# Three of a block's sixteen sums of silu(h) on GpSimd instead of VectorE, in a fused convolution and feed-forward kernel

## The chip, the cores and the metric

The kernel runs on one core of one Trainium2 chip. The metric is the device time of one execution in microseconds (us), inputs and outputs in the chip's main memory (HBM). A core has five engines that each work through their own list of instructions in order and meet only at semaphores: TensorE (PE in the profile; PEld is its loading of weights), VectorE (DVE), ScalarE (ACT), GpSimd (POOL) and SyncE (SP), which issues transfers. ScalarE and GpSimd can issue transfers too. Operands lie in SBUF, and TensorE's results in the eight banks of PSUM.

## What is computed

A light-weight convolution along the sequence with seven taps per head, softmax over the taps, and behind it a feed-forward layer with silu, all in float32:

```python
# x: 8 x 4096 x 192, weight: 8 heads x 7 taps
w = softmax(weight, axis=-1)
out[b, s, h, g] = sum over k of w[h, k] * x_pad[b, s + k, h, g]   # 6 zeros ahead of each sequence
# x = out as 32768 x 192; w_in: 192 x 2048, w_out: 2048 x 192
h = x @ w_in
g = h * (1.0 / (1.0 + np.exp(-h)))
return g @ w_out
```

## The kernel before

**Tiles.** The 32768 tokens are worked in NB = 32 blocks of 1024, each as two halves n of 512. The 192 features are three parts k of 64, and the 2048 hidden features are four groups j, each of two chunks a, with e the two 128-row pieces of a chunk. SBUF tiles of g (the silu of h) are [128, n, e, 512], one for each j and a.

**Fewer products.** From block 1 on the kernel doesn't multiply plainly. The up product (x @ w_in) is made of 15 products a group in place of 18 (`product`, L649, tokens P), whose right operands are sums of the block's features (`win`) and whose left operands are sums of the weights made at the start. ScalarE copies one accumulator out of PSUM (L698, tokens u), VectorE adds others to it (L692, tokens X, a, b), and ScalarE takes the silu (L710, tokens S). The down product (g @ w_out) is made in the same spirit, of seven forms in place of eight (`out_slot`, L765). Four of the forms need sums of g, made by `sum_g` (L733), four for each group j, so sixteen a block:

- t.j0 = g[0,1] - g[0,0], t.j1 = g[1,1] - t.j0, t.j2 = g[1,1] - g[0,1], t.j3 = g[1,0] - t.j1, where g[a,n] is chunk a, half n. Each is a subtraction of 128x1024 values.
- t.j0 and t.j1 share a tile `t`, t.j2 and t.j3 the next one. The pool of these tiles has three buffers.

The output products are tokens Di.je: slot i (0 to 5), group j, piece e. A slot is four products of 32 columns side by side. Slot 3 reads t.j2 (three of the four products) and t.j3, slots 4 and 5 read t.j0 and t.j3 and t.j3 alone, slot 2 reads t.j1, and slots 0 and 1 read g. So D3.00 and D3.01 are the readers of t.02, D3.10 and D3.11 of t.12, D3.21 and D3.20 of t.22.

**The convolution.** Taps of part k are tokens v.ki, i the tap (`conv`, L508 to L516), two blocks ahead of the output products that they stand among. Tap 0 is written by ScalarE (L508). For i from 1 to 6 and blocks from 4 on, ScalarE multiplies the shifted features by the tap into a buffer `u` (L511), and GpSimd issues a transfer that adds this buffer to the tile `nat` (L512, 256 KB read and written). Taps of one part add into the same tile, so each of these issues waits for the landing of the one before it in its part; and it waits in GpSimd's queue. A block has 18 of them. GpSimd also copies the six columns of the block before (`halo_in`, L498, or sets them to zero, L492). After the start it has no other work.

**The order.** `PLAN` is a list written out by hand: for every block, the tokens in the order in which they go to the engines' queues; a sign shifts a token to the block before (-) or after (+). `step` turns a token into instructions, and `pin` keeps their order in each queue. Only a few, the halo copy among them, are placed by the scheduler. `START` is the like list for the first block of this kind. The part of `PLAN` with the sums reads:

```
-P8.3 P5.0 v.02 -D1.00 =st.3 -t.00 -b5.3 -a0.2 -a0.3 -sp.2 -D1.30 u5.4 -a0.1 -D1.01
v.22 v.12 -D0.00 -S0.3 v.23 -D0.31 -D1.10 -t.01 -t.03 -D2.00 -sp.0 -b5.2 -t.02 -D4.01
-S1.2 -S5.2 -D5.00 -D2.01 v.03 -D5.01 -D3.00 -S0.1 -t.10 -D1.20 -D4.00 v.13 v.24
-D3.01 -t.11 -D2.11 -D2.10 -t.13 -D5.11 v.14 -D4.10 v.04 -D0.21 -S1.3 -w.0 -w.1 -S0.2
v.25 -t.20 -S5.4 -t.21 -D5.10 -D4.11 +ld.2 -D1.21 -D0.30 -D0.11 -t.23 -S5.3 -D4.20
-D5.20 -t.12 -D3.10 -D3.11 -D2.21 -D2.20 -D0.20 -D4.21 -t.22 -D3.21 v.05 -D1.31 -D5.21
-t.30 -D0.01 -w.2 -t.31 -t.33 -D5.31 -D1.11 v.15 v.26 +i.2 u5.0 -D0.10 -z1.0 -t.32
```

Ahead of it stand v.01, v.10 and v.11, and before these, at the end of the list, +v.21. The last block's output products are in `finish`.

Of the kernel before, what the change touches and what calls it, by code (L numbers as in the profile page):

```python
# [12 lines left out]
ALU = mybir.AluOpType  # L13
# [4 lines left out]
def kernel(  # L18
# [24 lines left out]
    nc = tc.nc  # L43
# [13 lines left out]
    NB = NT // TT  # L57
# [109 lines left out]
    def pin(ins):  # L167
        return tc.keep_in_program_order(ins)
# [549 lines left out]
    def sum_g(b, j, i):  # L718

        t = sums.setdefault((b, j), {})  # L720
        if i // 2 not in t:
            t[i // 2] = tpool.tile([P, 2, 2 * TB], F32, tag="t", name="t")

        def of(a, n):
            return gs[b, j, a][:, n, :, :].rearrange("p e t -> p (e t)")

        u, v = (
            (lambda: (of(0, 1), of(0, 0))),
            (lambda: (of(1, 1), t[0][:, 0, :])),
            (lambda: (of(1, 1), of(0, 1))),  # L730
            (lambda: (of(1, 0), t[0][:, 1, :])),
        )[i]()
        pin(nc.vector.tensor_tensor(t[i // 2][:, i % 2, :], u, v, op=ALU.subtract))  # L733

    def out_slot(b, j, i, e, half=None):

# [145 lines left out]
    def step(b, token):  # L882
# [19 lines left out]
        elif name[0] in "uXabS":  # L902
            sums_h(b, name, *digits)
        elif name == "t":
            sum_g(b, *digits)
        elif name[0] == "D":
            i, (j, e) = int(name[1]), digits
            for half in range(2) if i == 3 and b == NB - 1 else (None,):
                out_slot(b, j, i, e, half)
        elif name[0] in "Mzyx":  # L910
            merge(b, name, *digits)
        elif name == "o":
            turn_out(b, *digits)
        elif name == "st":
            store_out(b, *digits)
        elif name == "dp":
            next(downs)
        elif name == "cp":
            copy_plain(b, *digits)
        elif name == "go":  # L920
            pool.tensor_copy(warm, nats[1][:, digits[0], 0, 0:1])
            for g in (2, 3):
                for e in range(2):
                    combine(g, e)
        elif name == "ld":
            if b + 1 < NB:
                load(b + 1, digits)
        elif b + 1 < NB:
            {"i": turn_in, "ha": halo_in, "v": conv, "sp": spread, "w": win}[name](
                b + 1, *digits[: 1 + (name == "v")]  # L930
            )
# [204 lines left out]
```

## Time and profile before

| | |
|---|---|
| two timed runs | 2319.44 and 2320.99 us, median 2320.22 |
| span of the profiled execution | 2317.9 us |
| time of a block, from its first output product to the next block's | 71.19 us (blocks 5 to 29) |
| of it, output products | 36.2 us |
| busy: TensorE, VectorE, ScalarE, GpSimd | 2310.2, 1797.9, 1496.0, 534.9 us |
| sums (L733) | 496, 1.22 us each, all on VectorE |
| accumulating transfers (L512) | 504, 4.5 us from issue to landing in the median |

In the profile's rows a group of instructions is given by line, engine, operation and tiles (out<-in), and xN is their number. Timeline rows begin with the start and the duration in us from the start of the span; equal neighbours are merged, and in brackets stands how long the engine had been idle before and what ended that. A product in float32 has two records, so one Di.je is eight records. "PEclk" is the clock that TensorE was granted, as a share of full speed. In a row for a stretch of time the busy times of PE, PEld, DVE, ACT and POOL follow each other, then come PEclk, the transfers' share and GB/s.

### The profile page before, as it was taken

How to read it: one execution, taken by the hardware profiler on the slowest of the kernel's cores; microseconds unless marked ns; L12 is line 12 of the kernel's file. 1: busy time of each engine (PE TensorE's matmuls, PEld its weight loads, DVE VectorE, ACT ScalarE, POOL GpSimd, SP SyncE). 2: the span in 40 equal slices, each digit the busy share in tenths (PEclk: the TensorE clock that was granted, in tenths of full speed). 3: DMA queues.
4: the chain of work that ended last, by engine and by line, in shares of the span. 5: the costliest groups of instructions: out<-in, count | busy, mean ns of one | idle time of the engine just before them, and what ended most of it. 6: DMA issues, size and time to landing. Idle time of an engine off the chain costs nothing.

```text
span 2317.9 us, 45421 instructions
## 1 busy us (share of the span) xinstructions
PE 2310.2 (100%) x17630; PEld 949.6 (41%) x17630; DVE 1797.9 (78%) x2373; ACT 1496.0 (65%) x2779; POOL 534.9 (23%) x675
## 2 busy tenths in 40 slices
PE   9999999999999999999999999999999999999999
PEld 5454443444433344433444334443334443344433
DVE  8998777777777777777777777777777777777777
ACT  5347766677666686666776667866667666677543
POOL 4921112221122211222211222112221212221100
PEclk9999999999999999999999999999999999999999
DMA  7236557766567765677655676556776557765401
GB/s 159 58 62 101 98 100 118 123 115 102 95 113 120 121 105 93 109 120 121 110 98 99 115 124 117 102 93 113 119 123 108 94 104 120 120 114 93 81 17 25
DMA packets 522601, 238.81 MB, mean 103 GB/s; under 512 B 430368, under 2 KB 435488, under 8 KB 522384
## 3 DMA queue, kind: packets, MB, share of 16 engines
q0 software_dynamic: 73120, 133.89, 34.4%
q1 hardware_dynamic: 447392, 101.78, 25.0%
q8 instruction: 138, 2.26, 0.4%
q14 instruction: 79, 0.65, 0.1%
q10 hardware_dynamic: 1872, 0.23, 0.1%
HBM read 31.46 MB, written 25.17 MB: 24 GB/s over the span
## 4 chain that ended last, share of the span: by engine, by line
PE 89%; DVE 0%; issue 0%; ACT 0%; ACTq 0%
PE ps L765 45%; PE ps L649 39%; PE ps L666 5%; DVE cmb L175 0%; ACT u L175 0%; DVE osb L175 0%; ACTq L175 0%
## 5 line engine op out<-in xcount | busy, mean ns | idle before, releaser
L512 POOL DMA_DIRECT2D nat<-u x504 | 432.6, 947 | 1544.6 <-ACT u L511 1192.3
L765 PE MATMUL ps<-g,wo 128*32 128x512 f32 x2976 | 694.9, 592 | 0.0
L649 PE MATMUL ps<-win,wr 64*128 64x512 f32 x1550 | 688.7, 591 | 0.8 <-ACT yx L828 0.8
L649 PE MATMUL ps<-win,ws 64*128 64x512 f32 x1550 | 644.3, 589 | 0.0
L698 ACT COPY u<-ps 128x512 f32<-128x512 f32 x775 | 452.2, 587 | 166.8 <-PE ps L649 93.8
L765 PE MATMUL ps<-t,wo 128*32 128x512 f32 (+2 forms) x4528 | 538.5, 446 | 0.0
L765 PE MATMUL ps<-t,wx 128*32 128x512 f32 x2976 | 485.1, 592 | 0.0
L649 PE MATMUL ps<-dup,wr 64*128 64x512 f32 x868 | 425.6, 589 | 0.0
L511 ACT ACTIVATE u<-xt,taps 128x512 f32<-128x512 f32 x504 | 346.0, 715 | 44.0 <-DMA nat<-u 43.6
L733 DVE TENSOR_TENSOR t<-g,t 128x1024 f32<-128x1024 f32 x248 | 303.3, 1223 | 89.7 <-PE ps L765 84.2
L692 DVE TENSOR_TENSOR g<-u,ps 128x512 f32<-128x512 f32 x465 | 312.2, 682 | 72.2 <-PE ps L649 58.8
L649 PEld LDWEIGHTS ps<-win,wr 64*128 64x128 f32 x1550 | 275.7, 187 | 217.1 <-issue 177.1
L733 DVE TENSOR_TENSOR t<-g 128x1024 f32<-128x1024 f32 x248 | 298.8, 1216 | 76.4 <-PE ps L765 56.7
L692 DVE TENSOR_TENSOR ps<-u,ps 128x512 f32<-128x512 f32 x310 | 215.7, 696 | 132.3 <-PE ps L649 62.0
L710 ACT ACTIVATE g<-ps 128x512 f32<-128x512 f32 x465 | 281.0, 604 | 48.6 <-PE ps L649 47.0
L649 PEld LDWEIGHTS ps<-win,ws 64*128 64x128 f32 x1550 | 258.8, 187 | 126.1 <-issue 103.9
L710 ACT ACTIVATE g<-g 128x512 f32<-128x512 f32 x465 | 281.4, 629 | 30.3 <-DVE g L692 30.3
L765 PEld LDWEIGHTS ps<-t,wo 128*32 128x32 f32 x4528 | 181.4, 110 | 239.2 <-issue 227.6
L649 PE MATMUL ps<-dup,ws 64*128 64x512 f32 x682 | 271.9, 589 | 0.0
L831 ACT COPY cmb<-ps 96x512 f32<-96x512 f32 x30 | 17.4, 581 | 393.1 <-PE ps L765 393.1
L765 PE MATMUL ps<-g,wx 128*32 128x512 f32 x1488 | 245.9, 594 | 0.0
L765 PEld LDWEIGHTS ps<-g,wo 128*32 128x32 f32 x2976 | 170.4, 110 | 130.6 <-issue 129.8
(93 smaller groups left out, 2015.1 us busy)
## 6 DMA issues: line engine op xcount, KB each, us to landing
nat<-u POOLq DMA_DIRECT2D x504, 256.0 KB, 4.5
dup<-nat SPq DMA_DIRECT2D x345, 128.0 KB, 2.5
nat<-in_x_dram SPq DMA_DIRECT2D x382, 64.0 KB, 4.4
out_dram<-osb SPq DMA_DIRECT2D x376, 64.0 KB, 2.0
raw<-in_moe_w_out_dram SPq DMA_DIRECT2D x8, 384.0 KB, 3.7
raw<-in_moe_w_in_dram SPq DMA_DIRECT2D x12, 192.0 KB, 4.8
ws<-wr POOLq DMA_DIRECT2D x8, 192.0 KB, 4.8
raw<-in_moe_w_in_dram SPq DMA_DIRECT2D x6, 128.0 KB, 3.1
```

What stands on the lines that cost most here:

```text
L511: pin(nc.scalar.activation(z, src, AF.Copy, scale=tap))
L512: pin(nc.gpsimd.dma_start(out=dst, in_=z, accum_op=ALU.add))
L649: nc.tensor.matmul(to[:, cols], raw(g, *LEFT[e][r], e), rhs[:, cols], start=first, stop=True, skip_group_check=True,)
L666: nc.tensor.matmul(plain_bank(b, n and 1 + e)[:, cols], rows(wr[j] if own == e else ws[j], e)[:, a, k, :], rows(dups[b], e)[:, SLOT[e][2 * ...
L692: pin(nc.vector.tensor_tensor(out_, u, v, op=op))
L698: pin(nc.scalar.copy(us[b, g, o][:, cols], t1[:, cols]))
L710: pin(nc.scalar.activation(h, src, AF.Silu))
L733: pin(nc.vector.tensor_tensor(t[i // 2][:, i % 2, :], u, v, op=ALU.subtract))
L765: nc.tensor.matmul(accs[b][at][SQ * q : SQ * q + SQ, to], lhs[:, e, SQ * k : SQ * k + SQ], rhs[:, e, ts(q, TB // 4) if i == 5 else to], st ...
L831: pin(nc.scalar.copy(c[0], acc[0][0:n, :]))
```

## The change

In `sum_g` the sums t.02, t.12 and t.22 (i == 2, groups 0 to 2) of blocks 2 to 30 go to GpSimd. Their tokens keep their places in the list, and nothing else is changed.

```diff
@@ sum_g
             (lambda: (of(1, 1), of(0, 1))),
             (lambda: (of(1, 0), t[0][:, 1, :])),
         )[i]()
-        pin(nc.vector.tensor_tensor(t[i // 2][:, i % 2, :], u, v, op=ALU.subtract))
+        engine = nc.gpsimd if 1 < b < NB - 1 and i == 2 and j != 3 else nc.vector
+        pin(engine.tensor_tensor(t[i // 2][:, i % 2, :], u, v, op=ALU.subtract))
```

After the edit the lines behind L733 have numbers higher by one: the sums are L734, the output products L766. GpSimd's queue of one block reads, from the changed program: v.21, v.01, v.11, v.02, v.22, v.12, v.23, t.02, v.03, v.13, v.24, v.14, v.04, v.25, t.12, halo copy, t.22, v.05, v.15, v.26, v.06, v.16.

## The prediction

> **What bounds the kernel now.** I read the page first, then the waits of the changed line, then the timelines of TensorE, GpSimd and VectorE over one block.
>
> ```profile
> span 2317.9 us, 45421 instructions
> PE 2310.2 (100%) x17630; PEld 949.6 (41%) x17630; DVE 1797.9 (78%) x2373; ACT 1496.0 (65%) x2779; POOL 534.9 (23%) x675
> PE 89%; DVE 0%; issue 0%; ACT 0%; ACTq 0%
> ```
>
> TensorE bounds it: busy 2310.2 of 2317.9 us, and the chain that ended last is TensorE nearly throughout. No other engine sets the pace, so taking work from VectorE can bring at most the 7.7 us that TensorE is not busy. The changed line says the same from its side:
>
> ```profile
> L733 DVE TENSOR_TENSOR t<-g x248: 1181/1218/1227, 139.0 to 2295.1; 128x1024 f32<-128x1024 f32 x124
> who waited for it (us, times):
>   ACT nat L508: 6.1, 1
>   PEld ps L765: 1.2, 4
> ```
>
> A sum takes VectorE 1.22 us, and in the whole run TensorE waited 1.2 us for sums. What counts is whether GpSimd delivers the three sums before TensorE asks for them. This is block 15: TensorE's first output product (D1.00), then the first products that need t.02, t.12 and t.22 (D3.00, D3.10, D3.21); then VectorE's sums; then GpSimd's queue.
>
> ```profile
> 1136.90 0.63 PE L765 MATMUL ps<-g,wx 128*32 128x512 f32 x3
> 1145.09 1.04 PE L765 MATMUL ps<-t,wo 128*32 128x512 f32 x8
> 1156.90 1.04 PE L765 MATMUL ps<-t,wo 128*32 128x512 f32 x8
> 1162.05 1.04 PE L765 MATMUL ps<-t,wo 128*32 128x512 f32 x8
> ```
>
> ```profile
> 1141.60 1.22 DVE L733 TENSOR_TENSOR t<-g 128x1024 f32<-128x1024 f32 x1
> 1144.77 1.23 DVE L733 TENSOR_TENSOR t<-g,t 128x1024 f32<-128x1024 f32 x1
> 1147.90 1.23 DVE L733 TENSOR_TENSOR t<-g,t 128x1024 f32<-128x1024 f32 x1 [1.91 <-PE ps L765]
> ```
>
> ```profile
> 1132.46 0.88 POOL L512 DMA_DIRECT2D nat<-u  x1 [12.97 <-ACT u L511]
> 1137.35 2.60 POOL L512 DMA_DIRECT2D nat<-u  x3 [4.01 <-ACT u L511]
> 1143.53 0.86 POOL L512 DMA_DIRECT2D nat<-u  x1 [3.58 <-ACT g L710]
> 1146.61 1.72 POOL L512 DMA_DIRECT2D nat<-u  x2 [2.23 <-ACT u L511]
> 1148.95 0.84 POOL L512 DMA_DIRECT2D nat<-u  x1 [0.61 <-ACT g L710]
> 1155.46 2.59 POOL L512 DMA_DIRECT2D nat<-u  x3 [3.39 <-DMA nat<-u]
> 1157.08 1.19 POOL L498 COPY xt<-tail 64x18 f32<-64x18 f32 x1
> ```
>
> The sum t.02 is done on VectorE at 1142.82, 2.27 us before D3.00 at 1145.09. GpSimd is only 23% busy, but its queue is in order, and it is a queue of waits: each accumulating transfer of the convolution (L512) waits until the one before it in its feature part has landed. In the order of the list the issues are v.21, then v.01 (1132.46); v.11, v.02, v.22 (the three from 1137.35); v.12 (1143.53); v.23 and v.03 (the two from 1146.61); v.13 (1148.95); v.24; and v.14, v.04, v.25 (the three from 1155.46), then the halo copy. The token -t.02 stands between v.23 and v.03, -t.12 behind v.25, and -t.22, as the changed program's GpSimd queue has it, behind the halo copy and ahead of v.05.
>
> **The change part by part.** It moves 87 sums: three in each of blocks 2 to 30. Tiles, readers and the instruction orders of TensorE, ScalarE and SyncE stay.
>
> Removed from VectorE: 87 x 1.22 = 106 us of busy time. This is worth nothing: TensorE waited 1.2 us for sums in all, so I count a gain of 0.
>
> The price of one sum on GpSimd. The trace has no subtraction of 1024 elements there, but it has smaller ones, undisturbed, one behind the other:
>
> ```profile
> 111.75 0.45 POOL L175 TENSOR_TENSOR ws<-wr,ws 64x128 f32<-64x128 f32 x1
> 112.17 0.45 POOL L175 TENSOR_TENSOR ws<-wr 64x128 f32<-64x128 f32 x1
> 120.74 0.60 POOL L175 TENSOR_TENSOR wx<-wo,wx 128x192 f32<-128x192 f32 x1
> 121.29 0.60 POOL L175 TENSOR_TENSOR wo<-wo 128x192 f32<-128x192 f32 x1
> ```
>
> From start to start that is 0.42 us at 128 elements and 0.55 at 192: 0.13 per 64. Carried on to 1024 (832 more than 192, 13 times 64) it is 0.55 + 13 x 0.13 = 2.24; the spans (0.45, 0.60) give 0.60 + 13 x 0.15 = 2.55. Bounds: not under VectorE's own 1.22, not over 0.55 x 1024/192 = 2.93, where nothing would be fixed cost. I take 2.3, nearest to the start-to-start slope.
>
> Sum t.02. It starts when the issue of v.23 is over, 1146.61 + 0.86 (the row of v.12 has 0.86 for one issue) = 1147.47, and ends at 1149.77. D3.00 wanted it at 1145.09: TensorE stands 4.68 us in this block, and everything behind it in TensorE's order with it. Nothing earlier in the block moves, since v.23 hangs on v.22's landing, and v.22 on ScalarE's work of the block's up products, all before the stall. So the stall comes anew in each block that still has transfers in the queue, and that is blocks 2 to 29: the 504 issues below, 18 a block; in block 30 nothing stands ahead of t.02. The mean over those 28 pairs of rows, (start of v.23) + 0.84 + 2.3 - (start of D3.00), is 4.86; the first and the last pair are these, and give 5.59 and 3.87.
>
> ```profile
> nat<-u POOLq DMA_DIRECT2D x504, 256.0 KB, 4.5
> ```
>
> ```profile
> 218.30 1.04 PE L765 MATMUL ps<-t,wo 128*32 128x512 f32 x8
> 220.75 1.72 POOL L512 DMA_DIRECT2D nat<-u  x2 [3.50 <-ACT u L511]
> 2141.72 1.04 PE L765 MATMUL ps<-t,wo 128*32 128x512 f32 x8
> 2142.45 1.73 POOL L512 DMA_DIRECT2D nat<-u  x2 [2.74 <-ACT u L511]
> ```
>
> 28 x 4.86 = 136 us. With the bounds 1.22 and 2.93 of one sum it is 106 to 154.
>
> Sum t.12. Behind t.02 wait v.03 and v.13: issued at 1149.8 and 1150.3, so v.13 is 1.4 later than before; v.14, which waits for v.13's landing, goes from 1155.46 to 1156.8, v.25 behind it is over at 1158.05 + 1.4 = 1159.4, and t.12 ends at 1161.7. D3.10 now asks at 1156.90 + 4.68 = 1161.6. That is a tie; over the blocks I count 0.1 each, 3 us (bounds 0 and 1.3, if every landing slips as far as v.13's issue).
>
> Sum t.22. The halo copy ends 1158.27 - 1158.05 = 0.2 after the last issue, so t.22 ends near 1161.7 + 0.2 + 2.3 = 1164.2; D3.21 asks at 1162.05 + 4.8 = 1166.9. Hidden by 2.7 us. What is queued behind it, v.05 and its kind, moves by less than TensorE does, so the next block sees it no later.
>
> VectorE during t.02: its next sum, t.13 at 1147.90, waits for TensorE (D4.00, which stands behind D3.00) and slides with the stall, so after 1146.00 VectorE does nothing that could disturb GpSimd. Count 0.
>
> The clock. A stall of 4.9 us is new to this kernel, and TensorE's clock answers to idleness. At the end of the run TensorE's last work ends at 2307.32 + 4.92 = 2312.24, and the clock falls:
>
> ```profile
> 2307.32 4.92 PE L765 MATMUL ps<-t,wo 128*32 128x512 f32 x97
> 2313.00:2318.00 5.00, 0.00 (x0) 0.00 (x0) 1.28 (x4) 0.37 (x1) 0.00 (x0) 0.82 0.40 66
> 1.14 3.78 PE L435 MATMUL ps<-zeros 128*128 128x256 f32 x8 [1.14 <-DVE warm L175]
> 5.25 1.16 PE L435 MATMUL ps<-zeros 128*128 128x256 f32 x4
> ```
>
> The granted clock (the column of 0.82) means 1.8 of those 5 us at 0.5, so it fell at 2316.2, after 3.9 us of idleness. At the start of the run the same matmuls take 0.47 us each (3.78/8) and later 0.29 (1.16/4): TensorE is slow for about 4.1 us (1.14 to 5.25) after a rest. A fall would thus cost half of 4.1 us, 2.05. One fall after 3.9 us does not tell how often a stall of 3.9 to 5.6 brings one; the bounds are none and all 28 (0 and 57 us), and I take the middle, 29. The Trainium skill (TensorE: Matmul & The Clock Gate, Part 1) says that the gate looks at free-running windows of about 3.4 us and halves the clock after an idle one. By it a stall of 4.9 us holds a whole window in (4.9 - 3.4)/3.4 = 44% of its positions, 12 of 28 blocks, an estimate of 25 us in place of 29; the 3.9 us of the row agree with it.
>
> The sum: 2317.9 + 136 + 3 + 29 = 2486 us of span. The two timed runs have a median of 2320.2, 2.3 above this profiled execution's span, so 2488.
>
> **The rivals.**
> (a) The clock never falls: the stalls are too short or fall badly for it. For it speaks that the only fall seen came at 3.9 us, not below; against it that most stalls here are longer. 2320 + 139 = 2459.
> (b) The clock falls in every block: 2320 + 139 + 57 = 2516.
> (c) VectorE and GpSimd keep each other out of SBUF. At the start of the run this is visible: the same 64x128 operation that takes 0.45 us alone takes 1.17 beside a VectorE operation of 1.21.
>
> ```profile
> 46.91 1.17 POOL L175 TENSOR_TENSOR wr<-wr,ws 64x128 f32<-64x128 f32 x1
> 45.42 1.21 DVE L175 SCALAR_TENSOR_TENSOR two<-raw,two 128x768 int32<-128x768 int32 x1
> ```
>
> Were t.02 and t.12 each held for one VectorE sum (1.22), that is 28 x 2.44 = 68 us more, and the longer stalls would fetch the clock down nearly always: 2516 + 68 = 2584. Against it stands that VectorE itself waits for TensorE while t.02 runs. The Trainium skill (SBUF — State Buffer, Who interferes with whom) says that a VectorE instruction with two SBUF inputs and a GpSimd one that reads SBUF exclude each other for the whole instruction; the row agrees.
> (d) Not slower: v.22 lands early, so that v.23 leaves early. This one place decides: v.22, the third of the issues from 1137.35 to 1139.95, begins at about 1139.1, and a landing takes
>
> ```profile
> DMA to landing us min/median/max: 3.2/4.5/8.2
> ```
>
> 3.2 us at least. v.23 at 1142.3 would still end t.02 at 1145.4, 0.35 after D3.00: 28 x 0.35 = 10 us, 2330. To cost nothing, v.23 must leave before 1141.9. Against it: v.23 leaves after D3.00 began in the blocks shown, first and last included.
>
> **How the numbers follow.** The stall with some falls of the clock 0.58 (own range 2465 to 2512), (a) 0.18, (b) 0.12, (c) 0.07, (d) 0.05. The forecast is the first, 2488 us. The range 2448 to 2530 holds the first, (a) and (b), with about 10 us for the price of the sum; (c) and (d), 0.12, are left out. A measurement of this kernel can tell about 2% from no change, which is 2274 to 2367: only (d) lies there. Slower 0.95; same 0.04; faster 0.01, since TensorE's idle time is 0.3% of the span.
>
> **What would show it.** The profile after should have TensorE idle before L766 with GpSimd's t as its releaser, 28 times near 4.9 us, at D3.00 alone; blocks some 76 to 77 us apart where they were 71.2; GpSimd sums of 2.2 to 2.6 us; and granted-clock stretches of 0.5 behind a part of the stalls. I am wrong if TensorE waits at D3.10 or D3.21 as well (the queue's later sums then matter), if the sums take over 3 us (then the port), if the stalls fade from block to block (then the transfers adapt), or if the queue reaches t.02 by 1142.

## The result, and the profile after

The changed kernel takes 2632.09 us (2630.63 and 2633.55) against 2320.22: ratio 1.1345, 95% interval 1.1312 to 1.1378. It is slower, as forecast, but by 312 us and not by 168, and outside the range of 2448 to 2530.

The page of the changed kernel, with its span, its engines and the chain that ended last:

```profile
span 2628.9 us, 45657 instructions
PE 2419.2 (92%) x17630; PEld 980.7 (37%) x17630; DVE 1844.3 (70%) x2286; ACT 1495.2 (57%) x2779; POOL 754.2 (29%) x762
PE 56%; DVE 11%; issue 10%; DMA 6%; POOL 4%; ACT 3%; POOLq 0%; DVEq 0%; ACTq 0%
```

The chain was TensorE at 89% and is now TensorE at 56%, with VectorE, transfers and GpSimd in it. TensorE's busy time rose by 109 us for the same 17630 records: part of its work ran slowly. VectorE's busy time rose too, by 46 us, with 87 instructions fewer. Both are signs that the waits alone don't explain. TensorE's waits (total, times, longest):

```profile
PE ps L766 <- POOL t L734: 131.6, 28, 5.9
PE ps L766 <- DVE t L734: 70.5, 32, 2.9
```

28 waits for GpSimd's sums were forecast; 32 waits for VectorE's sums were not. Block 11 shows all of it. Its first output product starts at 950.30, and the next block's 82.05 us later, where it was 71.19. TensorE (in brackets the idle time before, and what ended it):

```profile
958.26 0.40 PE L766 MATMUL ps<-t,wo 128*32 128x128 f32 x8
963.28 1.93 PE L766 MATMUL ps<-t,wo 128*32 128x512 f32 x8 [4.61 <-POOL t L734]
964.98 1.07 PE L766 MATMUL ps<-g,wx 128*32 128x512 f32 x3
976.57 1.03 PE L766 MATMUL ps<-t,wx 128*32 128x512 f32 x6
980.08 2.55 PE L766 MATMUL ps<-t,wo 128*32 128x512 f32 x25 [2.48 <-DVE t L734]
```

D3.00 starts at 963.28 after 4.61 us of idleness. Its eight records then take 1.93 us where they took 1.04, and those behind it 1.07 in place of 0.6. The second wait is inside D4.20: three of its four products run (the row of 976.57), the fourth needs t.23 and comes at 980.08. The same block by stretches (us, busy PE, PEld, DVE, ACT, POOL, then the granted clock):

```profile
963.30:968.40 5.10, 5.10 (x25) 1.16 (x29) 0.00 (x0) 1.34 (x3) 2.49 (x3) 0.50 0.97 163
968.40:976.60 8.20, 8.20 (x95) 2.63 (x90) 7.82 (x5) 0.00 (x0) 7.86 (x6) 1.00 0.66 112
```

The slow products are those under a clock of 0.50. VectorE and GpSimd in this block:

```profile
958.15 1.23 DVE L734 TENSOR_TENSOR t<-g,t 128x1024 f32<-128x1024 f32 x1
968.64 1.23 DVE L734 TENSOR_TENSOR t<-g,t 128x1024 f32<-128x1024 f32 x1 [9.26 <-PE ps L766]
970.50 3.75 DVE L550 TENSOR_TENSOR win<-win,dup 128x512 f32<-128x512 f32 x1
975.49 4.54 DVE L734 TENSOR_TENSOR t<-g,t 128x1024 f32<-128x1024 f32 x2
```

```profile
960.00 0.84 POOL L512 DMA_DIRECT2D nat<-u  x1 [3.32 <-DVE t L734]
960.56 2.66 POOL L734 TENSOR_TENSOR t<-g 128x1024 f32<-128x1024 f32 x1
970.77 2.92 POOL L734 TENSOR_TENSOR t<-g 128x1024 f32<-128x1024 f32 x1
974.33 3.28 POOL L734 TENSOR_TENSOR t<-g 128x1024 f32<-128x1024 f32 x1
```

GpSimd issues v.23 at 960.00 and does t.02 behind it, until 963.22: the queue, as worked out. But while it does t.12 (970.77 to 973.69), VectorE's sum of window features takes 3.75 us in place of 0.69, and while it does t.22 (974.33 to 977.61), t.21 and t.23 take 4.54 in place of 2.45. The groups of VectorE over the run say the same; these were 1.22, 1.22 and 0.70 us on average:

```profile
L734 DVE TENSOR_TENSOR t<-g,t 128x1024 f32<-128x1024 f32 x248 | 374.5, 1511 | 265.0 <-PE ps L766 253.7
L734 DVE TENSOR_TENSOR t<-g 128x1024 f32<-128x1024 f32 x161 | 248.8, 1547 | 156.3 <-PE ps L766 103.5 <-ACT g L710 52.7
L550 DVE TENSOR_TENSOR win<-win,dup 128x512 f32<-128x512 f32 x31 | 40.5, 1305 | 1.1
```

Put against the starts of the same products before, as means over blocks 5 to 28, TensorE loses 4.91 us at D3.00, 2.4 more between D3.00 and D4.20 (slow work), and 3.7 from D4.20 to the next block: 11.0 a block, and 28 of them are 307 of the 311 us of span. The trace's clock records have 35 slow stretches behind waits: one behind D3.00 in each of the 28 blocks, and seven behind D4.20's wait. These seven, some 12 us, are in the 3.7.

### The profile page after: what moved, and what is told of

The parts are those of the page before. It is cut to its first block, busy times and chain, and to the rows that moved or that the text cites. A ratio compares the mean times of both kernels' runs of the same rounds, so it can differ in the third digit from the quotient of the medians.

```text
span 2628.9 us, 45657 instructions
## 1 busy us (share of the span) xinstructions
PE 2419.2 (92%) x17630; PEld 980.7 (37%) x17630; DVE 1844.3 (70%) x2286; ACT 1495.2 (57%) x2779; POOL 754.2 (29%) x762
## 4 chain that ended last, share of the span: by engine, by line
PE 56%; DVE 11%; issue 10%; DMA 6%; POOL 4%; ACT 3%; POOLq 0%; DVEq 0%; ACTq 0%
PE ps L766 26%; PE ps L649 26%; DVE t L734 8%; DMA nat<-u 6%; PE ps L666 4%; POOL t L734 3%; ACT g L710 2%; POOL nat L512 1%; DVE win L550 1%; ACT u L511 1%; DVE ps L692 1%; DVE osb L854 1%; ACT u L698 0%; DVE cmb L175 0%; DVEq L734 0%
## 5 line engine op out<-in xcount | busy, mean ns | idle before, releaser
L512 POOL DMA_DIRECT2D nat<-u x504 | 449.4, 1059 | 1638.5 <-ACT u L511 1398.9
L766 PE MATMUL ps<-t,wo 128*32 128x512 f32 (+2 forms) x4528 | 655.1, 482 | 196.6 <-POOL t L734 131.6
L766 PE MATMUL ps<-g,wo 128*32 128x512 f32 x2976 | 720.4, 601 | 0.0
L734 DVE TENSOR_TENSOR t<-g,t 128x1024 f32<-128x1024 f32 x248 | 374.5, 1511 | 265.0 <-PE ps L766 253.7
L766 PE MATMUL ps<-t,wx 128*32 128x512 f32 x2976 | 504.1, 613 | 5.5 <-DVE t L734 5.5
L766 PEld LDWEIGHTS ps<-t,wo 128*32 128x32 f32 x4528 | 216.6, 114 | 514.9 <-issue 264.3
L734 DVE TENSOR_TENSOR t<-g 128x1024 f32<-128x1024 f32 x161 | 248.8, 1547 | 156.3 <-PE ps L766 103.5
L766 PE MATMUL ps<-g,wx 128*32 128x512 f32 x1488 | 270.0, 645 | 0.0
L766 PEld LDWEIGHTS ps<-g,wo 128*32 128x32 f32 x2976 | 182.1, 111 | 221.9 <-issue 220.8
```

Of the source, the lines that this page charges most:

```text
L512: pin(nc.gpsimd.dma_start(out=dst, in_=z, accum_op=ALU.add))
L734: pin(engine.tensor_tensor(t[i // 2][:, i % 2, :], u, v, op=ALU.subtract))
L766: nc.tensor.matmul(accs[b][at][SQ * q : SQ * q + SQ, to], lhs[:, e, SQ * k : SQ * k + SQ], rhs[:, e, ts(q, TB // 4) if i == 5 else to], st ...
```

## The experiments

Theory A has three terms a block: the wait behind GpSimd's queue, work at half clock after it, and VectorE shut out of SBUF while GpSimd's later sums read there. Rivals: the slow products have another cause than the clock's fall; VectorE is late only since everything has slid; the amount of work moved counts and not its place. Unless said otherwise an experiment's diff is against the changed kernel. All times, with the ratio to the kernel before measured beside them:

| run | us | ratio (95%) |
|---|---|---|
| e1: t.02 alone on GpSimd | 2523.84 | 1.0878 (1.0847 to 1.0910) |
| e2: t.12 and t.22 alone | 2459.16 | 1.0599 (1.0569 to 1.0630) |
| e3: all three, TensorE kept at work | 2585.70 | 1.1145 (1.1113 to 1.1177) |
| e4: all three, t.02 moved forward | 2443.75 | 1.0533 (1.0502 to 1.0564) |
| e5: t.02 alone, moved forward | 2336.35 | 1.0071 (1.0056 to 1.0086) |
| e6: t.22 alone | 2327.62 | 1.0033 (1.0022 to 1.0044) |
| e7: all three, t.12 and t.22 as memsets | 2521.23 | 1.0867 (1.0845 to 1.0889) |
| e8: all three, t.02 and t.12 moved forward | 2371.75 | 1.0235 (1.0211 to 1.0259) |
| e9: t.02 and t.12 | 2542.27 | 1.0958 (1.0926 to 1.0990) |
| e10: t.02 alone, TensorE kept at work in part | 2489.31 | 1.0729 (1.0688 to 1.0771) |

**The first sum alone (e1).**

```diff
-        engine = nc.gpsimd if 1 < b < NB - 1 and i == 2 and j != 3 else nc.vector
+        engine = nc.gpsimd if 1 < b < NB - 1 and i == 2 and j == 0 else nc.vector
```

> Only t.02 goes to GpSimd; t.12 and t.22 are back on VectorE. Theory A (three terms a block: 4.9 us stall of TensorE at D3.00 behind GpSimd's queue, some 2.4 us of work at half clock behind it, some 3.1 us at D4.20 because VectorE's sums are kept out of SBUF while GpSimd makes t.12 and t.22): the third term goes, the first two stay, 28 x 7.3 us, about 2525 us. Theory C (VectorE is late at D4.20 only because the stall has moved everything, not because of GpSimd's reads): the wait at D4.20 stays, about 2600 us or more.

Measured: 2523.84 us. TensorE's only waits of weight are these, and D4.20 waits no more:

```profile
PE ps L766 <- POOL t L734: 128.4, 28, 5.7
```

A block loses 4.77 us at D3.00 and 2.5 behind it. VectorE's work has slid by the same 7.3 us as in the changed kernel and still delivers in time, so sliding alone does not make t.23 late. The third term hangs on t.12 and t.22.

**The later two alone (e2).** The same line with `j in (1, 2)`.

> Only t.12 and t.22 go to GpSimd; t.02 is back on VectorE. Theory A: nothing holds TensorE at D3.00, but now t.12, behind v.25 in the queue and 2.65 us long, ends near 23.9 us after the block's first output product where D3.10 asks at 20.0: about 4 us of stall there and half clock behind most of them, 2475 to 2505 us. A rival without a price for the clock: 2430 to 2440 us. If the queue only hurts t.02: 2320 us.

Measured: 2459.16 us, below the 2475 to 2505 of theory A and above the rival without a clock.

```profile
PE ps L766 <- POOL t L734: 72.6, 22, 4.1
PE ps L766 <- POOL xt L492: 22.3, 6, 4.9
```

All 28 waits are at D3.10 (the second row names the memset of the halo behind the sum). It starts 3.7 us later than before, and 1.3 are lost behind it: the clock fell in 17 of the 28 blocks. The sum t.12 is in time in the changed kernel only because the first wait has already held TensorE back.

**TensorE kept at work during the wait (e3).**

```diff
+        for _ in range(5 if 1 < b < NB - 2 and (i, j, e) == (3, 0, 0) else 0):
+            pin(
+                nc.tensor.matmul(
+                    accs[b][at],
+                    w[:, 0, 0, 0:P],
+                    gs[b, j, 1][:, 0, 0, :],
+                    start=True,
+                    stop=True,
+                    skip_group_check=True,
+                )
+            )
         for q in range(4):
             lhs, rhs = forms[own if q < NP else other]()
```

> The changed kernel, with five products of 0.86 us on operands that lie ready put ahead of D3.00 into its accumulator in blocks 2 to 29, so that TensorE works through the stall; D3.00 then starts the accumulator afresh. Theory A: D3.00 comes no later than before, the clock stays full, and with 2.4 us less delay VectorE's later sums meet GpSimd's at other moments, so that D4.20 waits under 1 us: 2470 to 2500 us. If the slow products behind the stall have another cause than the rest (weights, transfers, waits): 2600 us or more, since the added products save nothing.

Measured: 2585.70 us. Half of the expectation held: D3.00 starts 4.96 us late as before, and between it and D4.20 nothing more is lost, where 2.4 us were. So those 2.4 us are the clock's. The other half failed: D4.20 still waits, now at full clock ahead of it.

```profile
PE ps L777 <- DVE t L734: 70.1, 28, 3.8
PE ps L777 <- POOL t L734: 8.3, 18, 1.3
```

What t.23 of VectorE went through in block 11, and GpSimd's t.12 and t.22 beside it:

```profile
957.27 5.90 DVE L734 TENSOR_TENSOR t<-g,t 128x1024 f32<-128x1024 f32 x1 [0.57 <-PE ps L777]
```

```profile
956.72 5.36 POOL L734 TENSOR_TENSOR t<-g 128x1024 f32<-128x1024 f32 x2
```

A sum of 1.23 us took 5.90: it came in after t.12 had begun and was let in only after t.22. In this program the scheduler placed the short halo copy ahead of t.12 and not between the two as in the changed kernel, so t.22 follows t.12 directly. I had counted one GpSimd sum in its way. This wait alone brought the clock down in 18 blocks.

**GpSimd writes and doesn't read (e7).**

```diff
-        pin(engine.tensor_tensor(t[i // 2][:, i % 2, :], u, v, op=ALU.subtract))
+        if engine is nc.gpsimd and j:
+            for _ in range(3):
+                pin(engine.memset(t[i // 2][:, i % 2, :], 0.0))
+        else:
+            pin(engine.tensor_tensor(t[i // 2][:, i % 2, :], u, v, op=ALU.subtract))
```

> The changed kernel, with t.12 and t.22 of GpSimd replaced by three memsets each into the same half tile, some 2.9 us that write SBUF and read nothing (these sums are left out of the result). t.02 stays. Theory A with a lock on reads: VectorE's sums keep their 1.22 us, D4.20 waits no more, and the time is that of the first sum alone, 2515 to 2535 us. If any GpSimd work in SBUF holds VectorE: VectorE's sums of 3 us and more stay, and 2600 to 2630 us.

Measured: 2521.23 us, the time of the first sum alone (2523.84). GpSimd's memsets, 0.95 us each, and VectorE's sums beside them:

```profile
L736 POOL MEMSET t<- x174: 941/951/2045, 232.2 to 2425.3; 128x1024 f32 x174
```

```profile
L738 DVE TENSOR_TENSOR t<-g,t 128x1024 f32<-128x1024 f32 x248 | 303.5, 1224 | 288.2 <-PE ps L770 282.8
L738 DVE TENSOR_TENSOR t<-g 128x1024 f32<-128x1024 f32 x161 | 196.5, 1223 | 176.5 <-PE ps L770 123.5 <-ACT g L710 52.9
```

At the same places, and about as long, GpSimd's writes leave VectorE at 1.22 us. It is the reading that shuts VectorE out; this is called the lock below. The Trainium skill (SBUF — State Buffer, Who interferes with whom) says just that: a VectorE instruction with two SBUF inputs contends with a GpSimd instruction that reads SBUF, not with one that only writes it. The runs agree: 1511 and 1547 ns with reads, 1224 and 1223 without.

**The third sum alone (e6).** The line of the change with `j == 2`.

> Only t.22 on GpSimd, at its place behind the halo copy: from about 21.5 to 24.1 us after the block's first output product, where D3.21 asks at 25.15. If a late result is all that counts: 2320 us. If GpSimd's reads shut VectorE out: t.30 (22.0 before) begins at 24.1, t.33 ends near 28.4 in place of 26.6, and D5.31, which asks at 27.95, waits about 0.5 us: some 2335 us, and t.30 of VectorE shows 2 to 3.5 us in place of 1.22.

Measured: 2327.62 us, a small loss, with an interval clear of 1. Its result is in time, and yet 0.26 us a block are lost, all at D5.31, where VectorE's t.33 is late; the longest VectorE sum takes 3.93 us. Direction and place as the lock has it, the size half of what I had counted.

**The first two (e9).** The line of the change with `j < 2`.

> t.02 and t.12 on GpSimd, t.22 back on VectorE. In the changed kernel t.12 and t.22 stood one behind the other and shut VectorE out of t.23 and of the sum before it. Theory A, with t.12 alone in the way: t.23 ends about 27.6 us after the block's first output product, D4.20 asks at 26.2, so D4.20 waits some 1.4 us in place of 2.9, and the time is about 2590 us (2560 to 2600). If one GpSimd sum shuts VectorE out as long as two: 2632 us. If it is t.22 alone that does it: 2525 us.

Measured: 2542.27 us, less than expected: t.12 costs 18 us on top of the first sum, and t.22 the other 90, though t.22's own result is never late. The 18 are what is left of more: the slow work behind D3.00 cost 1.9 us a block here and 2.5 in e1. In block 11 VectorE's window sum still takes 3.84 us beside t.12, but then t.20, t.21 and t.23 follow unhindered, and D4.20 waits 12 times in the run, 5.3 us in all. (The halo copy stands three issues later here, so it no longer follows t.12.) One GpSimd sum is for the most part absorbed there; the second in a row is not.

**The first sum moved forward (e4, e5).** The diff of e4; e5 has the line of e1 as well.

```diff
-        "v.22 v.12 -D0.00 -S0.3 v.23 -D0.31 -D1.10 -t.01 -t.03 -D2.00 -sp.0 -b5.2 -t.02 -D4.01 "
+        "v.22 -t.02 v.12 -D0.00 -S0.3 v.23 -D0.31 -D1.10 -t.01 -t.03 -D2.00 -sp.0 -b5.2 -D4.01 "
```

> All three sums on GpSimd, but the token of t.02 stands ahead of v.12 instead of behind v.23, so t.02 begins some 3 us after the block's first output product and not 10. Theory A: no stall at D3.00; t.12 is then late by some 4 us as in the run with the later two sums alone, 2475 to 2505 us. If the sum is late for another reason than its place in the queue: D3.00 waits as in the changed kernel, about 2630 us.

> Only t.02 on GpSimd, with its token ahead of v.12. Queue theory: t.02 begins near 3.0 us after the block's first output product and ends by 7.0 even when a VectorE sum goes first, ahead of D3.00 at 8.19: 2320 us, or up to 2346 if GpSimd goes first and VectorE's t.03 comes late for D4.01 by up to 0.9 us. If GpSimd's sums cost TensorE time wherever they stand (by SBUF, or by the delay of the transfers behind them): 2370 us or more.

Measured: 2443.75 us for all three (e4) and 2336.35 for t.02 alone (e5). With its token two places up in GpSimd's queue, t.02 costs 16 us and not 204; TensorE never waits for it. So the place in the queue is the cause of the first wait. e4 lies under its range because the clock fell in only 10 blocks; it loses 3.4 us a block at D3.10, near the 3.7 of e2. The 16 us left in e5 fit the lock once more: VectorE's sums last up to 3.87 us there, and t.03 comes late for D4.01.

**Both moved (e8).** The same, and -t.12 ahead of v.14.

> All three sums on GpSimd, the token of t.02 ahead of v.12 and that of t.12 ahead of v.14 (behind v.24), t.22 in place. If the places in GpSimd's queue are what costs: t.02 and t.12 are in time (t.12 near 18 us where D3.10 asks at 20.0), D4.20 waits perhaps 0.2 us because t.23 lets GpSimd pass, and D5.31 about 0.5 us behind t.22: 2320 to 2345 us. If the amount of work moved is what costs, whatever its places: 2440 us, as with t.02 moved alone.

Measured: 2371.75 us, over my 2345 and far under 2440 (one of the four timed runs took 2383.53). GpSimd's results are in time, and what is left is VectorE: 1.5 us a block, and 8.1 in block 29, the only one in which the wait at D4.20 brought the clock down. In block 11, VectorE's t.01 and t.03, and GpSimd's t.02:

```profile
868.55 4.84 DVE L734 TENSOR_TENSOR t<-g,t 128x1024 f32<-128x1024 f32 x2
```

```profile
869.56 2.73 POOL L734 TENSOR_TENSOR t<-g 128x1024 f32<-128x1024 f32 x1
```

Two sums of 2.45 us take 4.84. Later t.21 takes 4.1 us beside t.12, and D4.20 waits for t.23 behind it.

**Half of the idleness filled (e10).** The diff of e1, and that of e3 with 2 products in place of 5.

> The kernel with the first sum alone on GpSimd, and two products of 0.86 us on ready operands ahead of D3.00 into its accumulator (blocks 2 to 29), which D3.00 then starts afresh. TensorE's idleness in a block falls from 4.6 to about 2.9 us, with D3.00 no earlier. Clock theory (the clock falls only when a whole stretch of 3.4 us, fixed in time, is idle): it never falls, and what remains is the wait itself, 28 x 4.9: 2450 to 2460 us. If any stall of a few us brings the clock down: 2524 us as without the products.

Measured: 2489.31 us: neither. TensorE's waits are now 2.0 to 3.8 us, and the clock fell in 16 of 28 blocks. Two of them, block 24 (a wait of 2.50 us) and block 20 (2.01), and the 6 us behind each:

```profile
1921.78 0.64 PE L777 MATMUL ps<-t,wo 128*32 128x512 f32 x4 [2.50 <-POOL t L734]
1614.29 0.64 PE L777 MATMUL ps<-t,wo 128*32 128x512 f32 x4 [2.01 <-POOL t L734]
```

```profile
1921.80:1927.80 6.00, 6.00 (x41) 1.66 (x45) 1.79 (x2) 1.82 (x3) 3.09 (x5) 0.72 0.95 159
1614.30:1620.30 6.00, 6.00 (x64) 2.05 (x68) 3.15 (x4) 1.94 (x4) 2.52 (x3) 1.00 1.01 167
```

A wait of 2.50 us brought the clock down (0.72 over the 6 us), so a fall needs no 3.4 us of idleness. In the six blocks with 2.3 us or less it never fell; in the 22 with 2.5 to 3.8 it fell in 16.

The clock records tell what decides. Within a run, all slow stretches begin on one grid of 3.413 us. Two stretches of that grid in e10, each with the one behind it:

```profile
1380.29:1383.70 3.41, 1.32 (x14) 0.43 (x18) 0.00 (x0) 2.24 (x5) 3.41 (x3) 1.00 1.12 138
1383.70:1387.11 3.41, 3.41 (x23) 0.86 (x19) 0.61 (x1) 1.22 (x2) 1.19 (x2) 0.50 1.07 183
1226.69:1230.10 3.41, 1.37 (x16) 0.47 (x20) 0.00 (x0) 2.36 (x5) 3.41 (x3) 1.00 1.20 140
1230.10:1233.51 3.41, 3.41 (x40) 1.02 (x36) 1.91 (x3) 1.28 (x2) 1.14 (x2) 1.00 1.06 176
```

In the first TensorE is idle for 2.09 us, and half clock follows; in the third it is idle for 2.04, and full clock stays. So it is throughout: the changed kernel, e1 to e4 and e7 to e10 have 181 falls, each behind a stretch with 2.02 us of idleness or more, and none of the 6111 other stretches at full clock has over 2.04. Within each run the two groups do not overlap.

## Why the prediction was wrong, point by point

**TensorE bounds the kernel, and VectorE's relief is worth nothing: right.** No run gained, not even those in which GpSimd's sums are in time.

**The price of a sum: right within its bounds.** 2.3 us by the slope of the smaller operations; t.02 measured 2.66, in the trace's spans, with the tail of an issue in it. t.12 and t.22 took 3.08 and 3.06 on average, so the sign "over 3 us (then the port)" showed.

**Sum t.02: right.** 4.86 us a block at D3.00 were worked out from GpSimd's queue, and D3.00 is 4.91 late, in the 28 blocks named. e5 shows that the queue is the cause.

**Sums t.12 and t.22: right for their results, wrong for what they do to others.** TensorE waits at neither D3.10 nor D3.21. But the step "VectorE during t.02 ... Count 0" was made for t.02 alone. For t.12 and t.22 I asked only whether TensorE would find them ready, and not which of VectorE's sums stood in SBUF at that time. With all three on GpSimd, this is the largest of the missing terms: 3.7 us a block from D4.20 on, 103 us (some 12 of them slow clock behind D4.20's wait), counted at 0. By e7 it is the lock on reads, and by e9 it needs t.22 behind t.12. Rival (c) had the lock, but with GpSimd as the one that is held, which lengthened its sums only from 2.66 to about 3.1, and with a chance of 0.07. That VectorE would be held, for up to two GpSimd sums in a row, was not in it. The two rows that (c) shows are no pair, besides: the VectorE operation from 45.42 is over at 46.63, ahead of GpSimd's at 46.91. Beside that one ran the next,

```profile
46.67 1.09 DVE L175 SCALAR_TENSOR_TENSOR mh<-mh,two 128x768 f32<-128x768 int32 x1
```

which is over at 47.76, while GpSimd's, 0.45 us long alone, ends at 48.08.

**The clock: right as a mechanism, half in size.** I took the middle, 14 falls at 2.05 us, 29 us. The clock fell behind the wait at D3.00 in all 28 blocks and cost 2.4 us each, 66 us: twice the falls, and each somewhat dearer. e3 shows that the term is the clock's. Rival (b) had this with a chance of 0.12, at 57 us. The estimate of 12 falls that hung on a wholly idle window of 3.4 us failed: by the traces about 2.0 us of idleness inside one stretch of the grid are enough. So a wait of 4.1 us or more cannot miss, since wherever it lies one stretch has half of it, and the 4.6 us or so of idleness at D3.00 brought a fall each time. Between 2.0 and 4.1 us it hangs on where the wait lies: at D3.00 and D3.10 the shortest wait that brought a fall had 2.44 us (e4), the longest that brought none 3.71 (e2).

The sum as measured: 28 x (4.9 + 2.4 + 3.7) = 308 us, on 2320: 2628 of the 2632. What stays open is the size of the lock's term in each run: e3, e6, e8 and e9 all came out otherwise than I had worked out from one block, by 7 us (e6) to 86 us (e3), since it depends on which VectorE instructions meet GpSimd's sums. The recorded starts alone don't tell which of the two is held: in block 11 the window sum starts at 970.50, ahead of t.12 at 970.77, and yet ends behind it.

## What to carry to other kernels

Before a step goes to another engine, place it in that engine's queue and ask when the instruction ahead of it is released: an engine that is 23% busy can still be late by 5 us, if it spends its time waiting for landings. Then ask what its reads keep from others: a GpSimd sum whose own result was hidden cost 90 us behind another one, and 7 alone, through the VectorE sums that it held up. And count a new wait of TensorE with the half clock behind it: here it came whenever some 2.0 us of idleness fell into one stretch of 3.41, and behind D3.00 it cost half as much again as the wait.

## What the runs showed of the hardware that was not expected

- TensorE's clock fell to 0.50 exactly where a stretch of the 3.413 us grid had about 2.0 us or more of idleness (181 falls; least 2.02 with a fall, most 2.04 without), and so in 28 of 28 blocks after waits of 3.8 to 5.7 us (e1). The slow stretches behind waits last 3.41 or 6.83 us in the clock records, nothing between. In e1 their starts are 78.51 us apart, 23 times 3.413, from block 4 to block 29.
- VectorE's recorded time holds its wait for SBUF: sums of 1.22 us are shown with up to 7.1 us, so the engine looks busier (46 us more, with 87 instructions fewer) though it does less.
- Two GpSimd sums directly one behind the other let no waiting VectorE sum through between them: in 27 of 28 blocks of e3 one lasted 5.2 to 7.1 us. With the halo copy between the two, in the changed kernel, a VectorE instruction got through in 18 of 28.
- A GpSimd subtraction of 128x1024 takes 2.66 us undisturbed, 2.2 times VectorE's; a memset of the same size 0.95.
